# First layer of the last two chunks by seven block products in place of eight

## The chip, the cores and the metric

One core of one Trainium2 chip. The metric is the device time of one execution in microseconds (us). Before the change three runs took 883.08, 883.62 and 883.85 us, median 883.62.

## The reference

Attention with 8 heads of width 64 over 8 sequences of 576 tokens (half of the heads see the last 32 keys, the others every 32nd key), and then two matrix products with a softplus between them over all 4608 tokens:

```python
def _moe_ref(x, w_in, w_out):          # x: 4608 x 512
    h = x @ w_in                       # w_in: 512 x 2048
    g = np.maximum(h, 0.0) + np.log1p(np.exp(-np.abs(h)))
    return (g @ w_out).astype(np.float32)   # w_out: 2048 x 512
```

Every product runs as three products of rounded parts: with `a = a_high + a_low`, `a*b` is `a_high*b_high + a_low*b_high + a_high*b_low`.

## The kernel before

The tokens are cut into nine chunks of 512 (`c` = 0 to 8), the 2048 hidden columns into 16 slices of 128 (`f`). One pair (c, f) is a step, and its work is:

- `hidden(c, f)` on TensorE (PE): 4 blocks of the 512 inputs x 3 part products = 12 matmuls of 128x128 by 128x512 into one bank `ph_c_f`. Two banks alternate. In the plan this task is `F` and the step's number, 16c + f: F102 is `ph_6_6`, F106 is `ph_6_10`.
- `log_part` on ScalarE (ACT): three instructions (Abs, Exp, Ln) from `ph` into `u_c_f`.
- `softplus` on VectorE (DVE): one SCALAR_TENSOR_TENSOR, max(ph, 0) + u. It is the last reader of the bank; F of the step after next writes there.
- `g_high` (a CAST to the rounded part) and `g_low` (TENSOR_TENSOR, u minus the high part), on DVE.
- `output(c, f)` on PE: 4 blocks of 128 tokens x 3 = 12 matmuls into four banks `py`, two steps behind `hidden`. After f = 15 `result` copies each bank out (ACT and DVE in turn) and stores it.

The attention of sequence b, in four pairs of heads n = 4b to 4b + 3, lies between the steps of the chunks before. `head_scores(n)` is `S{n}` on PE; the weighted sums of pair n - 1 go with it (`po`, `pv`; `pv` takes a `ph` bank). DVE adds the mask, takes maxima, subtracts, sums, normalizes and transposes in 16 pieces (`prob_transposes`); ACT takes the exponentials. `x_part` writes the result as `x_h` (ACT) and `x_l` (DVE), a ring of 1536 tokens per block of 128 inputs: chunks 6, 7 and 8 lie in it together. The last pair's sums, `V31`, stand alone.

The first part of the program (chunk 0) has its order by hand (`FIRST`). From step 18 on a planner sets it: each task has an urgency, an engine, a cost and the tasks it follows; tasks take the earliest gap on their engine, and are emitted in the order of planned starts. Each engine then works through its own queue strictly in that order. What stands where is fixed by

```python
pair_at[NFC * (b - 1) - 2 + 4 * i] = NPAIR * b + i   # step at which S{n} goes
...
for i in range(begin, len(steps) + LAG):             # LAG = 2
```

GpSimd (POOL) works only in chunk 0. The weights w_in stay in SBUF as `w_i_f`, high and low part side by side.

Of the kernel before, what the change touches and what calls it, by code (L numbers as in the profile page):

```python
# [76 lines left out]
class Plan:  # L77
# [39 lines left out]
def attention_softplus_ffn(  # L117
# [164 lines left out]
    def load_v(n):  # L282
        b, pair = order[n]
        if n < NPAIR:

            t = room[n]
        else:
            t = v_in
        t = t[:, : 2 * NTILE * D].rearrange("p (a c) -> p a c", c=2 * D)
        src = v[b, pair]  # L290
        nc.sync.dma_start(t[PAD:P, 0], src[0:TILE])
        src = src[TILE - PAD : 2 * TILE]
        src = bass.AP(
            tensor=src.tensor,
            offset=src.offset,
            ap=[src.ap[0], [TILE * 2 * D, NTILE - 1], src.ap[1]],
        )
        nc.sync.dma_start(t[:, 1:NTILE], src)
        vs[n] = t.rearrange("p a (h d) -> p a h d", d=D)
# [350 lines left out]
    def hidden(c, f, pairs=range(NPAIR)):  # L650
        n = CH[c]
        if 0 in pairs:
            phs[c, f] = ps_h.tile([P, 512], F32, tag="ph", name=f"ph_{c}_{f}")[:, :n]
        ph = phs[c, f]
        t0 = START[c] % RING
        i = 3 * pairs[0]
        for cc in (PAIRS[pair] for pair in pairs):
            for half, x in ((0, "h"), (1, "h"), (0, "l")):
                nc.tensor.matmul(  # L659
                    ph,  # L660
                    lhsT=w32["i", f][:, half, cc * P : (cc + 1) * P],
                    rhs=x_of(x, cc)[:, t0 : t0 + n],
                    start=(i == 0),
                    stop=(i == 3 * NCC - 1),
                )
                i += 1

    def log_part(c, f, steps=range(3)):
        if 0 in steps:
            us[c, f] = u_pool.tile([P, 512], F32, tag="u", name=f"u_{c}_{f}")[:, : CH[c]]  # L670
            nc.scalar.activation(us[c, f], phs[c, f], AF.Abs)  # L671
        u = us[c, f]
        if 1 in steps:
            nc.scalar.activation(u, u, AF.Exp, scale=-1.0)  # L674
        if 2 in steps:
            nc.scalar.activation(u, u, AF.Ln, bias=1.0)  # L676

    def softplus(c, f):
        u = us[c, f]
        nc.vector.scalar_tensor_tensor(  # L680
            u, in0=phs.pop((c, f)), scalar=0.0, in1=u, op0=ALU.max, op1=ALU.add
        )

    def g_high(c, f, engine=nc.vector):
        g = g_pool.tile([P, 512], F32R, tag="gh", name=f"gh_{c}_{f}")[:, : CH[c]]
        ghs[c, f] = g
        copy_on(engine, g, us[c, f])

    def g_low(c, f, engine):
        g = g_pool.tile([P, 512], F32R, tag="gl", name=f"gl_{c}_{f}")[:, : CH[c]]  # L690
        gls[c, f] = g
        engine.tensor_tensor(g, us.pop((c, f)), ghs[c, f].bitcast(F32), op=ALU.subtract)  # L692

# [35 lines left out]
    def task(name, fn, *args):  # L729
        first[name] = lambda: fn(*args)  # L730
# [132 lines left out]
    for i in range(begin, len(steps) + LAG):  # L863
        if i < len(steps):
            c, f = steps[i]
            w, x = CH[c] / 384, when[i]
# [4 lines left out]
            after = [f"F{i}", f"l{i-2}"]
            add(f"A{i}", x + 2, "ACT", 1.5 * w, lambda c=c, f=f: log_part(c, f), after)
            add(f"u{i}", x + 3.7, "DVE", 0.55 * w, lambda c=c, f=f: softplus(c, f), [f"A{i}"])
            after = [f"u{i}", f"O{i-3}"]
# [12 lines left out]
        for t in range(nt):
            name = f"O{k}" if t == nt - 1 else f"O{k}.{t}"
            after = [f"l{k}", before] + ([f"y{k-1}.{t}"] if f == 0 else [])
            add(name, x + 0.01 * t, "PE", 0.7, lambda c=c, f=f, t=t: output(c, f, (t,)), after)  # L890
            before = name
            if k == len(steps) - 1 and t == nt - 1:

                for h, (e, engine) in enumerate((("DVE", nc.vector), ("ACT", nc.scalar))):
                    cols = slice(DM // 2 * h, DM // 2 * (h + 1))
                    fn = lambda c=c, t=t, engine=engine, cols=cols: result(c, t, engine, cols)
                    add(f"y{k}.{t}{h}", x + 0.7 * t + 0.7, e, 0.35, fn, [name])
            elif f == NFC - 1:
# [8 lines left out]
    for i, n in pair_at.items():  # L907
# [137 lines left out]
```

## Time and profile before

| | |
|---|---|
| median of three runs | 883.62 us (883.08 to 883.85) |
| span of the profiled execution | 882.3 us; its own device time is not listed apart from that, the median of the runs is 1.3 us above the span |
| PE busy | 872.7 us, 99% |
| DVE, ACT, POOL busy | 585.7, 403.0, 65.8 us |
| matmuls of `hidden` and `output` | 1152 + 576 each, of 3456 in all |
| bytes moved | 58.39 MB, mean 66 GB/s |

Each line of a view on groups gives a source line, engine and instruction, the tiles written and read, the shape and count, then the busy time in all and of one. A matmul counts as busy to the end of its pipeline, so that neighbours overlap: the distance of two starts says what one costs. A line of the chain gives a start, a length and what ran.

### The profile page before, as it was taken

The page shows a single profiled execution, that of the slowest core. Times are in us where ns is not written, and L with a number is a line of the kernel's source. Part 1 is how long each engine was busy: PE and PEld are TensorE (multiplying, and loading weights), DVE is VectorE, ACT ScalarE, POOL GpSimd, SP SyncE. Part 2 cuts the span into 40 slices and gives each one's busy share as a digit, 9 for nine tenths or more (in the row PEclk, how much of TensorE's full clock was granted, in tenths as well). Part 3 has the DMA queues.
Part 4 walks back from the last instruction along what each step waited for, and adds up shares of the span by engine and source line. Part 5 has one row for each costly group of instructions (what it writes and reads, how often), then busy time and mean ns, then how long its engine had stood idle before and what let it go on. Part 6 is the DMA issues. An engine that isn't in the chain of part 4 may idle for free.

```text
span 882.3 us, 16274 instructions
## 1 busy us (share of the span) xinstructions
PE 872.7 (99%) x6626; PEld 717.4 (81%) x6626; DVE 585.7 (66%) x1283; ACT 403.0 (46%) x742; POOL 65.8 (7%) x88
## 2 busy tenths in 40 slices
PE   7999999999999999999999999999999999999998
PEld 5887888888888888888888888888888888888886
DVE  7999977888766677777766676667767333333332
ACT  6988754443443443443443444444443333333332
POOL 6346540000000000000000000000000000000000
PEclk9999999999999999999999999999999999999999
DMA  9894202211211121111211121102100010001001
GB/s 327 289 351 140 63 30 92 61 46 45 93 45 45 44 75 32 45 45 46 81 43 45 45 93 45 40 24 79 54 19 18 1 48 0 1 1 48 1 0 48
DMA packets 50090, 58.39 MB, mean 66 GB/s; under 512 B 3168, under 2 KB 35296, under 8 KB 50016
## 3 DMA queue, kind: packets, MB, share of 16 engines
q1 hardware_dynamic: 49728, 57.03, 20.0%
q8 instruction: 52, 0.85, 0.4%
q10 hardware_dynamic: 288, 0.33, 0.1%
q14 instruction: 22, 0.18, 0.1%
HBM read 47.91 MB, written 9.44 MB: 65 GB/s over the span
## 4 chain that ended last, share of the span: by engine, by line
PE 93%; DMA 2%; DVE 2%; ACT 1%; issue 1%; POOL 0%; SPq 0%; ACTq 0%; POOLq 0%
PE py L699 43%; PE ph L659 42%; PE pv L555 2%; DMA ro<-in_moe_w_out_dram 2%; PE ps L373 2%; PE po L555 2%; PE po L373 1%; PE pt L525 1%; DVE pt L487 0%; DMA raw_q<-in_qk_dram 0%; ACT prob L453 0%; DVE early_h L258 0%; DVE u L680 0%; DVE a_o L630 0%; ACT early_h L258 0%
## 5 line engine op out<-in xcount | busy, mean ns | idle before, releaser
L699 PE MATMUL py<-w_o,gh 128*128 128x512 f32 x1152 | 358.0, 392 | 0.0
L659 PE MATMUL ph<-x_h,w_i 128*128 128x512 f32 x1152 | 355.4, 390 | 0.4 <-DVE u L680 0.4
L671 ACT ACTIVATE u<-ph 128x512 f32<-128x512 f32 x144 | 86.1, 599 | 396.4 <-PE ph L659 393.8
L659 PEld LDWEIGHTS ph<-x_h,w_i 128*128 128x128 f32 x1152 | 215.7, 188 | 46.0 <-POOL prob L476 0.8
L699 PEld LDWEIGHTS py<-w_o,gh 128*128 128x128 f32 x1152 | 214.2, 188 | 46.3
L659 PE MATMUL ph<-x_l,w_i 128*128 128x512 f32 x576 | 224.1, 389 | 0.0
L699 PE MATMUL py<-w_o,gl 128*128 128x512 f32 x576 | 224.1, 389 | 0.0
L680 DVE SCALAR_TENSOR_TENSOR u<-ph,u 128x512 f32<-128x512 f32 x144 | 99.2, 689 | 172.3 <-ACT u L676 170.7
L487 DVE STREAM_TRANSPOSE pt<-prob 32x192 f32<-32x192 f32 x448 | 140.2, 317 | 6.7
L699 PEld LDWEIGHTS py<-w_o,gl 128*128 128x128 f32 x576 | 108.1, 188 | 22.8
L659 PEld LDWEIGHTS ph<-x_l,w_i 128*128 128x128 f32 x576 | 108.1, 188 | 22.7
L692 DVE TENSOR_TENSOR gl<-u,gh 128x512 fp32r<-128x512 f32 x135 | 93.3, 691 | 10.6
L674 ACT ACTIVATE u<-u 128x512 f32<-128x512 f32 x144 | 91.1, 633 | 4.3
L676 ACT ACTIVATE u<-u 128x512 f32<-128x512 f32 x144 | 90.9, 632 | 4.4
L258 DVE CAST gh<-u 128x512 fp32r<-128x512 f32 x130 | 55.4, 426 | 10.8 <-DVE u L680 0.9
L432 DVE TENSOR_TENSOR prob<-ps,mask_b 128x384 f32<-128x384 f32 x28 | 15.6, 557 | 50.0 <-PE ps L373 48.5
L258 ACT COPY qT<-prob 128x576 f32<-128x576 f32 x26 | 33.2, 1278 | 1.5 <-DMA prob<-in_qk_dram 1.5
L447 ACT ACTIVATE prob<-prob 128x576 f32<-128x576 f32 x24 | 16.5, 687 | 38.0 <-DVE prob L441 38.0
L373 PEld LDWEIGHTS ps<-kT,qT 64*32 64x32 f32 x1344 | 23.3, 106 | 9.9 <-issue 9.2
L373 PE MATMUL ps<-kT,qT 64*32 64x64 f32 x1344 | 27.8, 220 | 0.0
L373 PE MATMUL po<-kT,qT 64*32 64x64 f32 x672 | 22.0, 227 | 0.0
L432 DVE TENSOR_TENSOR prob<-po,mask_b 128x192 f32<-128x192 f32 x28 | 10.0, 356 | 17.8 <-ACT x_h L593 17.8
(99 smaller groups left out, 512.9 us busy)
## 6 DMA issues: line engine op xcount, KB each, us to landing
v_in<-in_v_dram SPq DMA_DIRECT2D x28, 320.0 KB, 3.5
out_dram<-o SPq DMA_DIRECT2D x35, 256.0 KB, 2.1
ri<-in_moe_w_in_dram SPq DMA_DIRECT2D x16, 512.0 KB, 8.2
ro<-in_moe_w_out_dram SPq DMA_DIRECT2D x16, 512.0 KB, 8.7
kT<-in_qk_dram SPq DMA_DIRECT2D x28, 288.0 KB, 3.3
prob<-in_qk_dram SPq DMA_DIRECT2D x28, 288.0 KB, 2.7
v_in<-in_v_dram SPq DMA_DIRECT2D x28, 48.0 KB, 2.8
room<-in_v_dram SPq DMA_DIRECT2D x4, 320.0 KB, 6.0
```

The lines of the kernel that those rows point to most:

```text
L258: (engine.copy if engine is nc.scalar else engine.tensor_copy)(dst, src)
L373: nc.tensor.matmul(pss[n, part][to : to + 32, at : at + 64], lhsT=qT[head, c : c + 32], rhs=k_of(n)[head, c : c + 64], start=True, stop=True,)
L432: nc.vector.tensor_tensor(pv, sv, m, op=ALU.add)
L487: nc.vector.transpose(pt[32 * (i + c) : 32 * (i + c) + 32, h, a : a + hi - lo, 32 * i : 32 * i + 32,], src[:, lo:hi, 32 * c : 32 * c + 32],)
L555: nc.tensor.matmul(po[64 * h : 64 * h + 64, TILE * x : TILE * x + TILE], lhsT=vs[n][:, a, h, :], rhs=pt_of(n, a)[:, h, a % 2], start=True, ...
L659: nc.tensor.matmul(ph, lhsT=w32["i", f][:, half, cc * P : (cc + 1) * P], rhs=x_of(x, cc)[:, t0 : t0 + n], start=(i == 0), stop=(i == 3 * N ...
L671: nc.scalar.activation(us[c, f], phs[c, f], AF.Abs)
L674: nc.scalar.activation(u, u, AF.Exp, scale=-1.0)
L676: nc.scalar.activation(u, u, AF.Ln, bias=1.0)
L680: nc.vector.scalar_tensor_tensor(u, in0=phs.pop((c, f)), scalar=0.0, in1=u, op0=ALU.max, op1=ALU.add)
L692: engine.tensor_tensor(g, us.pop((c, f)), ghs[c, f].bitcast(F32), op=ALU.subtract)
L699: nc.tensor.matmul(py[t], lhsT=g[:, sl], rhs=w32["o", f][:, half], start=(f == 0 and n == 0), stop=(f == NFC - 1 and n == 2),)
```

## The change

The first layer of chunks 7 and 8, 2 x 16 x 12 = 384 matmuls, becomes a 2 x 2 block product: rows are the two chunks (X1 = chunk 7, X2 = chunk 8), inner blocks the two halves of the 512 inputs, columns slices f and f + 8. In eight rounds (f = 0 to 7) seven block products of 6 matmuls each stand in place of eight, in Winograd's form of Strassen's method. Products 1, 6, 7 and 4 add up in one PSUM bank (`bank_a0` or `bank_a1`, in turn), 2 goes to `bank_b`, 5 and 3 to `bank_c`. In between ACT copies the state of a bank to SBUF (`keep`: k1, k5, k2 after products 1, 5, 6) and DVE adds a bank to such a copy (`join`: j1, j2, j5 after products 2, 3, 7). j1 gives the hidden values of (7, f), j2 of (8, f), j5 of (8, f + 8), and the bank after product 4 those of (7, f + 8).

The block sums: of x once, 8 additions for each of two blocks (i = 0 on POOL; i = 1 on DVE but for two on POOL), then high parts on ACT and low parts on DVE (`Xh`, `Xl`; into `t1` and into parts of the ring no longer read); of the weights in each round, two additions of 128x512 and four of 128x256 on POOL (`ww`), two casts on ACT and two subtractions on DVE (`Wh`, `Wl`, into `ws`). Tiles of the attention are laid into four larger ones (`home_0` to `home_3`) so that these sums take their place at the end. The values of chunk 8 stay in the places of `w_i`, and its second layer comes at the end, block by block. The last sequence's pairs are three steps apart, not four.

```diff
-            pair_at[NFC * (b - 1) - 2 + 4 * i] = NPAIR * b + i
+            pair_at[NFC * (b - 1) - 2 + (4 if b < B - 1 else 3) * i] = NPAIR * b + i
...
-    steps = [(c, f) for c in range(NCHUNK) for f in range(NFC)]
+    steps = [(c, f) for c in range(CA) for f in range(NFC)]     # CA, CB = 7, 8
...
+    def bank_of(p, f):
+        return lend({"2": "b", "5": "c", "3": "c"}.get(p, f"a{f % 2}"))
+    def product(p, f):
+        bank = bank_of(p, f)
+        n = 0
+        for i in range(2):
+            for half, part in ((0, "h"), (1, "h"), (0, "l")):
+                nc.tensor.matmul(bank, lhsT=w_left(p, f, half, i), rhs=x_right(p, part, i),
+                    start=p in "125" and n == 0, stop=n == 5, ...)
...
+    def x_whole(what, i, engine):
+        h, low = (x_at(part, k, lo).bitcast(F32) for part in "hl")
+        engine.tensor_tensor(t, h, low, op=ALU.add)
+    def x_sum_low(p, i):
+        nc.vector.tensor_tensor(x_right(p, "l", i), sums_r[p, i], h, op=ALU.subtract)
+    def w_whole(r, f):
+        t = sums_c[r, f] = io_pool.tile([P, DM], F32, tag="io", name=f"ww_{r}_{f}")
+        nc.gpsimd.tensor_tensor(t, w[:, 0], w[:, 1], op=ALU.add)
+    def w_sum(p, f):
+        nc.gpsimd.tensor_tensor(out, a, b, op=op)
+    def w_sum_low(r, f):
+        nc.vector.tensor_tensor(ws[:, r, 1], sums_c.pop((r, f)), h, op=ALU.subtract)
+    def keep(s, p, f):
+        nc.scalar.copy(lend(s), bank_of(p, f))
+    def join(s, p, f, c, row):
+        nc.vector.tensor_tensor(t, bank_of(p, f), t, op=ALU.add)
+        phs[c, row] = t
...
+    for f in range(HALF):        # one round; some(n): n blocks of the second layer, 3 matmuls each
+        mul("1"); k1; mul("2"); j1; soft(CA, f)
+        some(1); mul("5"); k5; mul("6"); k2
+        some(1); mul("3"); j2; soft(CB, f)
+        some(1); mul("7"); j5; weights of round f + 1
+        some(3); mul("4"); soft(CB, f + 8); soft(CA, f + 8); some(2)
```

(The last block is the new loop in short; `soft` is the ACT and DVE work of a step.)

Up to the end of chunk 5 the queues read as before. Three places after that matter. `S30` and `V31` are the scores of pair 30 and the sums of pair 31; a name such as `ph_6_2_6460` is tile `ph_6_2` with a buffer number.

First, DVE behind `V31`. Before, `V31` came after F110, and in DVE's queue the softplus of step (6, 8) followed the transposes of pair 30:

```order
L487 STREAM_TRANSPOSE pt_98<-prob_103 32x6x32 x2
L487 STREAM_TRANSPOSE pt_98<-prob_103 32x3x32 x2
L680 SCALAR_TENSOR_TENSOR u_6_8_6798<-ph_6_8_6766,u_6_8_6798 128x512
L258 CAST gh_6_8_6826<-u_6_8_6798 128x512
L692 TENSOR_TENSOR gl_6_8_6840<-u_6_8_6798,gh_6_8_6826 128x512
```

Now `V31` comes between F104 and F105, and in the same queue the sums of x for i = 1 and two low parts stand ahead of it (`s12` and `s5` are the homes of the later copies, used for sums of x here):

```order
L836 TENSOR_TENSOR t1_6939<-xw_11_0_6473,t1_6939 128x512
L599 TENSOR_TENSOR x_l3_592<-pv_31_0_6908,x_h3_590 128x18x16
L599 TENSOR_TENSOR x_l3_592<-pv_31_1_6915,x_h3_590 128x18x16
L817 TENSOR_TENSOR xw_22_1_6962<-x_h3_590,x_l3_592 128x512
L817 TENSOR_TENSOR s12_6964<-x_h3_590,x_l3_592 128x512
L828 TENSOR_TENSOR xw_11_1_6855<-s5_6873,xw_11_1_6855 128x512
L828 TENSOR_TENSOR s5_6873<-xw_22_1_6962,s5_6873 128x512
L828 TENSOR_TENSOR xw_22_1_6962<-xw_22_1_6962,xw_11_1_6855 128x512
L828 TENSOR_TENSOR s12_6964<-s12_6964,xw_22_1_6962 128x512
L836 TENSOR_TENSOR t1_6939<-xw_11_1_6855,t1_6939 128x512
L836 TENSOR_TENSOR x_l1_526<-xw_22_1_6962,x_h1_507 128x512
L688 SCALAR_TENSOR_TENSOR u_6_8_6895<-ph_6_8_6859,u_6_8_6895 128x512
```

The softplus of (6, 8), F104's, has moved behind everything that follows `V31`, eleven instructions; F106 writes the bank that it reads.

Second, ACT in round 2. Before, chunk 7's steps followed one another:

```order
L671 ACTIVATE u_7_2_7252<-ph_7_2_7228 128x512
L674 ACTIVATE u_7_2_7252<-u_7_2_7252 128x512
L676 ACTIVATE u_7_2_7252<-u_7_2_7252 128x512
L671 ACTIVATE u_7_3_7295<-ph_7_3_7268 128x512
L674 ACTIVATE u_7_3_7295<-u_7_3_7295 128x512
```

Now the same queue has the end of the step (7, 9), then k1, k5, the step (7, 2) and k2:

```order
L684 ACTIVATE u_7_9_7441<-u_7_9_7441 128x512
L867 COPY s12_6964<-bank_a0_7194 128x512
L867 COPY s5_6873<-bank_c_7224 128x512
L679 ACTIVATE u_7_2_7496<-s12_6964 128x512
L682 ACTIVATE u_7_2_7496<-u_7_2_7496 128x512
L684 ACTIVATE u_7_2_7496<-u_7_2_7496 128x512
L867 COPY s12_6964<-bank_a0_7194 128x512
L858 CAST ws_7191<-ww_1_3_7505 128x512
```

In rounds 2, 4 and 6 k2 stands behind the three instructions of (7, f), which read what j1 writes; in the other rounds it stands ahead of them.

Third, POOL, which had nothing after chunk 0 (its last rows before):

```order
L645 TENSOR_TENSOR w_o_15_1758<-a_o_15_1616,w_o_15_1758 128x512
L258 COPY qT_99<-prob_103 128x576
L1040 UNCONDITIONAL_BRANCH
```

Now it ends with the weight sums, six a round:

```order
L842 TENSOR_TENSOR ww_0_4_7612<-w_i_4_610 128x512
L842 TENSOR_TENSOR ww_1_4_7623<-w_i_12_1215 128x512
L855 TENSOR_TENSOR ww_1_4_7623<-ww_1_4_7623 128x256
L855 TENSOR_TENSOR ww_1_4_7623<-ww_0_4_7612,ww_1_4_7623 128x256
L855 TENSOR_TENSOR ww_0_4_7612<-ww_1_4_7623,ww_0_4_7612 128x256
L855 TENSOR_TENSOR ww_0_4_7612<-ww_0_4_7612 128x256
```

With four buffers, those of round 4 take the places of round 2's, which `Wl` of round 2 reads last: they start at the end of round 1.

More of the change, by code (lines that the diff above doesn't have):

```diff
@@ L891, in attention_softplus_ffn @@
             before = name
[L892 to L898, printed above, removed]
+            if f == NFC - 1:
                 e, cost, engine = (("ACT", 0.5, nc.scalar), ("DVE", 0.6, nc.vector))[t % 2]
@@ L968, in attention_softplus_ffn, with on_pe, out_task @@
             add(f"v{n+1}", z + 2, "SP", 1.3, lambda n=n: load_v(n + 1), [made], 2.0)
+    SLOT = 0.234
+    HALF = NFC // 2
+    now = when[len(steps)]
+    chain = f"F{len(steps) - 1}"
+    def on_pe(name, slots, fn, after):
+        nonlocal now, chain
+        add(name, now, "PE", slots * SLOT - Plan.WAIT, fn, [chain] + after)
+        now, chain = now + slots * SLOT, name
+    def out_task(c, f, t):
+        name, own = f"O{c}.{f}.{t}", [f"l{c}.{f}"]
+        if c == CA - 1:
+            own = [f"l{NFC * c + f}"]
+        elif f == 0:
+            own.append(f"y{c-1}.{t}")
+        on_pe(name, 3, lambda: output(c, f, (t,)), own)
+        if f < NFC - 1:
+            return
+        if c == CB and t == TPC - 1:
+            for h, (e, engine) in enumerate((("DVE", nc.vector), ("ACT", nc.scalar))):
+                cols = slice(DM // 2 * h, DM // 2 * (h + 1))
+                fn = lambda engine=engine, cols=cols: result(c, t, engine, cols)
+                add(f"y{c}.{t}{h}", now, e, 0.35, fn, [name])
+            return
+        e, cost, engine = (("ACT", 0.6, nc.scalar), ("DVE", 0.7, nc.vector))[t % 2]
+        add(f"y{c}.{t}", now, e, cost, lambda: result(c, t, engine), [name])
@@ new lines, in soft_task @@
+    def soft_task(c, f, src, late=()):
+        n = f"{c}.{f}"
+        for step in range(3):
+            fn = lambda step=step: log_part(c, f, (step,))
+            add(f"A{step}.{n}", now + step, "ACT", 0.65, fn, [src] if step == 0 else [f"A{step-1}.{n}"])
+        add(f"u{n}", now + 3, "DVE", 0.75, lambda: softplus(c, f), [f"A2.{n}"])
+        add(f"h{n}", now + 3.7, "DVE", 0.45, lambda: g_high(c, f), [f"u{n}", *late])
+        add(f"l{n}", now + 4.2, "DVE", 0.75, lambda: g_low(c, f, nc.vector), [f"h{n}"])
@@ new lines, in x_task @@
+    def x_task(i):
+        e, engine = ("POOL", nc.gpsimd) if i == 0 else ("DVE", nc.vector)
+        cost = 1.45 if i == 0 else 0.75
+        near, far = ([f"L{last - 3 + 2 * i + k}{half}" for half in range(2)] for k in range(2))
+        z = when[i_of[last - 3 + 2 * i + 1]] + 6
+        free = [f"V{last}"]
+        start = [f"Y{last}0", f"Y{last}1", f"S{last}"] if i == 1 else []
+        whole = {"11": near, "12": near + start, "22": far, "21": far + start}
+        sums = {"5": ["11", "12"], "7": ["12", "22", "5"], "6": ["22", "5", "7"], "4": ["21", "6"]}
+        to = {"5": free, "6": ["12"], "7": [chain], "4": [chain]}
+        k = 0
+        for what in ("11", "22", "12", "21"):
+            fn = lambda what=what: x_whole(what, i, engine)
+            early = "POOL" if i == 1 and what in ("11", "12") else e
+            by = nc.gpsimd if early == "POOL" else engine
+            fn = lambda what=what, by=by: x_whole(what, i, by)
+            add(f"X{what}.{i}", z + k, early, 1.45 if early == "POOL" else cost, fn, whole[what])
+            k += 0.1
+        for p in ("5", "7", "6", "4"):
+            fn = lambda p=p: x_sum(p, i, engine)
+            add(f"X{p}.{i}", z + k, e, cost, fn, [f"X{q}.{i}" for q in sums[p]])
+            k += 0.1
+        for p in ("5", "6", "7", "4"):
+            after = [f"X{p}.{i}"] + [q if len(q) > 2 else f"X{q}.{i}" for q in to[p]]
+            late = 0 if p in "56" else now - z
+            add(f"Xh{p}.{i}", z + late + k, "ACT", 0.65, lambda p=p: x_sum_high(p, i), after)
+            after = [f"Xh{p}.{i}"]
+            add(f"Xl{p}.{i}", z + late + k + 1, "DVE", 0.75, lambda p=p: x_sum_low(p, i), after)
+            k += 0.1
@@ new lines, in w_task @@
+    def w_task(f, z):
+        since = [f"P6.{f-1}", f"W3.{f-1}"] if f else [f"F{len(steps) - 2}"]
+        for r in range(2):
+            add(f"W{r}.{f}", z, "POOL", 1.45, lambda r=r: w_whole(r, f), since)
+        before = [f"W0.{f}", f"W1.{f}"]
+        for p in ("5", "7", "6", "3"):
+            add(f"W{p}.{f}", z + 3, "POOL", 0.8, lambda p=p: w_sum(p, f), before)
+            before = [f"W{p}.{f}"]
+        used = {0: "63", 1: "57"}
+        for r, done in ((1, "7"), (0, "3")):
+            after = [f"W{done}.{f}"] + (
+                [f"P{p}.{f-1}" for p in used[r]] if f else [f"V{last}", f"S{last}"]
+            )
+            add(f"Wh{r}.{f}", z + 6, "ACT", 0.65, lambda r=r: w_sum_high(r, f), after)
+            add(f"Wl{r}.{f}", z + 7, "DVE", 0.75, lambda r=r: w_sum_low(r, f), [f"Wh{r}.{f}"])
@@ L969, in attention_softplus_ffn @@
+    for g in (HALF - 1, NFC - 1):
+        for t in range(TPC):
+            out_task(CA, g, t)
+    for t in range(TPC):
+        for f in range(HALF):
+            for g in (f, f + HALF):
+                out_task(CB, g, t)
     with tc.manual_schedule():
```

216 lines of the change are left out of this document (191 added, 25 removed).

## The prediction

> **What bounds the kernel now.** I read the page first, then stretches of the span, the chain that ended last and the waits.
>
> ```profile
> PE 872.7 (99%) x6626; PEld 717.4 (81%) x6626; DVE 585.7 (66%) x1283; ACT 403.0 (46%) x742; POOL 65.8 (7%) x88
> PEclk9999999999999999999999999999999999999999
> ```
>
> PE is busy for 99% of the span at its full granted clock. The stretches (busy us and instructions of PE, PEld, DVE, ACT, POOL, then clock, DMA share, GB/s) show where other engines have room:
>
> ```profile
> 640.00:690.00 50.00, 50.00 (x407) 41.03 (x408) 33.70 (x76) 18.69 (x31) 0.00 (x0) 1.00 0.06 16
> 784.00:832.00 48.00, 48.00 (x213) 39.77 (x212) 17.41 (x29) 17.06 (x28) 0.00 (x0) 1.00 0.06 22
> ```
>
> While attention runs DVE is busy for two thirds, in the last chunks for 36%; POOL does nothing in either. In the chain the last two chunks are matmuls and nothing else, and the wait list has, from chunk 1 on, no wait of PE that matters:
>
> ```profile
> 734.27 2.72 PE py L699 x12
> 736.99 2.72 PE ph L659 x12
> ...
> 870.27 8.17 PE py L699 x36
> ```
>
> ```profile
> PE ph L659 <- DVE u L680: 0.4, 1, 0.4
> ```
>
> Twelve matmuls take 2.72 us, so one takes a slot of 0.227. What removes a slot is worth a slot, as long as PE finds no new wait.
>
> **What it removes.** Eight rounds of seven products of 6 matmuls are 336, in place of 384: 48 slots, **-10.9 us**. Nothing else leaves PE: second layer, attention and the end (a copy in two halves and a store) keep their work. The two POOL sums for i = 1 end before V31 and cost nothing. No transfer is added; the loads of the last pairs come a few us earlier, which the same three-step spacing in chunk 1 bore without a wait of PE.
>
> **What it adds on the other engines.** The prices:
>
> ```profile
> L692 DVE TENSOR_TENSOR gl<-u,gh 128x512 fp32r<-128x512 f32 x135 | 93.3, 691 | 10.6
> L258 DVE CAST gh<-u 128x512 fp32r<-128x512 f32 x130 | 55.4, 426 | 10.8 <-DVE u L680 0.9
> L674 ACT ACTIVATE u<-u 128x512 f32<-128x512 f32 x144 | 91.1, 633 | 4.3
> L258 ACT COPY o<-py 128x512 f32<-128x512 f32 x19 | 10.2, 582 | 5.2 <-PE py L699 5.2
> L692 POOL TENSOR_TENSOR gl<-u,gh 128x512 fp32r<-128x512 f32 x9 | 12.2, 1355 | 7.8 <-DVE gh L258 5.1 <-PE ph L659 1.0 <-ACT gh L258 0.9
> ```
>
> A round has 66 slots (42 of products, 24 of second layer), 14.96 us. DVE's part in it: four steps of 0.69 + 0.43 + 0.69, three joins and two low parts of 0.69, 10.7 us; ACT's: four of 1.87, three copies and two casts of 0.6, 10.5 us; POOL's: two sums of 1.36 and four of half that (an estimate), 5.4 us. As sums all fit. What decides is the order in each queue and one contention.
>
> **The contention.** From chunk 0, where POOL worked beside DVE (start, us):
>
> ```profile
> 94.74 1.16 POOL L476 TENSOR_TENSOR prob<-prob,st 128x576 f32<-128x576 f32 x1
> ...
> 107.74 1.30 POOL L692 TENSOR_TENSOR gl<-u,gh 128x512 fp32r<-128x512 f32 x1 [0.98 <-PE ph L659]
> ```
>
> ```profile
> 94.71 0.69 DVE L680 SCALAR_TENSOR_TENSOR u<-ph,u 128x512 f32<-128x512 f32 x1 [1.08 <-ACT u L676]
> ...
> 107.87 1.72 DVE L630 SCALAR_TENSOR_TENSOR a_o<-ro,a_o 128x512 uint32<-128x512 uint32 x1
> ...
> 123.06 0.79 DVE L258 CAST w_o<-a_o 128x512 fp32r<-128x512 f32 x1
> ```
>
> ```profile
> 84.41 0.68 DVE L645 TENSOR_TENSOR w_o<-a_o,w_o 128x512 fp32r<-128x512 f32 x1
> 84.62 0.93 POOL L258 CAST gh<-u 128x512 fp32r<-128x512 f32 x1 [1.62 <-DVE u L680]
> 85.01 1.09 DVE L630 SCALAR_TENSOR_TENSOR a_o<-ro,a_o 128x512 uint32<-128x512 uint32 x1
> 85.52 1.73 POOL L645 TENSOR_TENSOR w_o<-a_o,w_o 128x512 fp32r<-128x512 f32 x1
> ```
>
> A DVE instruction with both inputs in SBUF takes 1.72 instead of 0.69 when POOL began first: it works only once POOL is through (107.87 + 1.72 - 0.69 = 108.90, so POOL held it 1.16). In the third block the two engines take turns, each lengthened by the other. A DVE instruction with one input in PSUM (94.71) keeps its 0.69. So I charge a whole POOL sum 1.16 and a half one 0.57 (estimate) to each such DVE instruction that meets it. The Trainium skill has this as a rule (SBUF — State Buffer, "Who interferes with whom"): a VectorE instruction with two SBUF inputs and a GpSimd one that reads SBUF exclude each other, and whoever issued first keeps the port for the whole instruction; the trace agrees (1.72 against 0.69). By that rule the sum is the one below; if nothing met, it would be the first rival's.
>
> In a round 13 of DVE's 17 instructions are of the exposed kind (the casts too: the one at 123.06 took 0.79 beside a POOL sum, against a mean of 0.426), and the six POOL sums of the round after next become ready exactly when `Wl` has freed their buffers, at the round's start.
>
> **Waits in the Strassen rounds.** Handoffs:
>
> ```profile
> 805.02 0.60 ACT L671 ACTIVATE u<-ph 128x512 f32<-128x512 f32 x1 [3.51 <-PE ph L659]
> ...
> 806.32 0.63 ACT L676 ACTIVATE u<-u 128x512 f32<-128x512 f32 x1
> ...
> 806.99 0.69 DVE L680 SCALAR_TENSOR_TENSOR u<-ph,u 128x512 f32<-128x512 f32 x1 [3.56 <-ACT u L676]
> ...
> 807.78 0.43 DVE L258 CAST gh<-u 128x512 fp32r<-128x512 f32 x1
> ...
> 808.31 0.69 DVE L692 TENSOR_TENSOR gl<-u,gh 128x512 fp32r<-128x512 f32 x1
> ```
>
> ACT to DVE costs 0.04, a dependent DVE instruction 0.1, three ACT instructions 1.95. Count from product 1's first slot. Product 7 starts at slot 39, 8.84 us, and needs k2; product 4 at slot 54, 12.24, and needs j5.
>
> *Even rounds (2, 4).* Product 4 of the round before ended at -1.4. Five ACT instructions end at 2.0 to 2.2; then DVE has two softplus, two casts, two low parts, and j1. Undisturbed, from the first of the two Ln at 1.4 (an instruction followed by an independent one costs 0.08 less than its time): 0.6 + 0.7 for the softplus, 0.7 the casts, 1.2 the low parts, 0.7 j1, end 5.3; the step (7, f) ends at 7.5, k2 at 8.1: hidden by 0.7. With POOL's two whole sums from 0.1 the first softplus waits to 2.6; the second, with a bank in PSUM, does not wait; then each cast (0.3 on the port) and low part (0.53) lets a half sum go first: 2.6 + 0.6 + 0.6 + 0.3 + 0.57 + 0.3 + 0.57 + 0.53 + 0.57 + 0.6 + 0.7 = 7.9 for j1, ACT 9.9, k2 10.5. Product 7 waits **1.7** in rounds 2 and 4 each, and all of PE's queue behind it, so that the wait is lost whole; on ACT a cast for the next weights and the step (8, f) stand behind k2 and come later by as much. Round 6 has no weight sums left to meet.
>
> *Odd rounds.* k2 comes first and is in time; j5 follows (7, f)'s low part at 12.0 against 12.24: no wait. Round 1 is the exception: its POOL queue holds two sets of sums (the second waits for stores of chunk 6's results), the second meets (7, 1). j1, late by the first set as above, ends at 8.5, ACT at 10.5; softplus, cast and low part each let a half sum go first, 10.9 + 0.53 + 0.57 + 0.3 + 0.57 + 0.6 + 0.7 = 14.1 for j5: **1.9**.
>
> *Round 0.* Count from F111's end: its own step and two low parts of weights keep DVE to 5.1. Four low parts of x follow, and alternate with the first set, 5.1 + 1.16 + 0.53 + 1.16 + 0.53 + 0.57 + 0.53 + 0.57 + 0.6 = 10.8, so that j1 ends at 11.5, not 8.3. k2 waits for the last of them and ends at 11.5 (product 7 was due at 11.4), (7, 0) on ACT at 13.5, its softplus, cast and low part at 15.4, j5 at 16.1; product 4 was due at 15.0: **1.3** with the little at product 7. k1, behind six casts, ends 6.3 after F111 and product 6 starts at 7.3: hidden.
>
> *After round 7.* (7, 15) leaves the bank with product 4; Abs to low part (0.2, five ACT instructions in the queue, softplus, two casts, two low parts) end at 5.4, PE comes to them after 20 slots, 4.5: **0.9** (0.5 to 1.1, by the dependent gaps).
>
> Bounds of the first three: 0 without a meeting; and if a half sum held the port as long as a whole one, four times 0.6 more a burst, of which I let half reach PE, 1.2 in each of four rounds.
>
> **Waits in chunk 6.** A pair's block on PE and DVE's work behind it, before:
>
> ```profile
> 151.06 0.41 PE ps L373 x20
> ...
> 153.19 2.94 PE py L699 x12
> ```
>
> ```profile
> 159.41 2.64 DVE L487 STREAM_TRANSPOSE pt<-prob 32x192 f32<-32x192 f32 x8
> ```
>
> The block takes 2.13 plus 0.22 on the next group, and the transposes begin 8.35 after it. They take 5.2 (16 at 0.33 by this row). Now all 16 stand ahead of F100's softplus, and F102, which writes its bank, stands after S30 and four groups, 2.13 + 2.94 + 3 x 2.72 = 13.2, first slot 13.1. Softplus ends at 8.35 + 5.2 + 0.7 = 14.2: already 1.1 late. POOL's sums of x for i = 0 start once pair 29's low parts are written, and hold up the subtraction and the low part of (6, 3): another 1.1. **2.2** (0 to 2.6).
>
> F106 waits for F104's softplus. From V31's end: a cast into `t1` 0.6, its low part 0.6, two low parts of 0.36, sums 0.6 to 0.8 each (six, three of them dependent, 4.2), two low parts 1.2, softplus 0.7: 8.2 with the handoffs. PE has F105 and one output group in between, 2.94 + 2.72 - 0.16 = 5.5. **2.8**; the ACT side alone (F105's three, two casts, low part, softplus, 4.7 after F105's end against 2.7) makes it 2.0 at least; 3.2 at most if POOL's last sum is late.
>
> **The sum.** -10.9 + 2.2 + 2.8 + 1.3 + 1.9 + 3.4 + 0.9 = +1.6 us against the profiled 882.3; on the median of 883.62, **885.2 us**. All low ends (-10.9 + 2.0 + 0.5) give 875.2; all high ends (-10.9 + 2.6 + 3.2 + 6.6 + 4.8 + 1.1 = +7.4) 891.
>
> **Rivals.** *The two engines seldom meet on the path.* If POOL is done before DVE's burst, only the waits written in the order stay: -10.9 + 1.1 + 2.8 + 0.9 = -6.1, **877.5**, the other side. For it: DVE has 4 us of free time a round; against: the buffers tie POOL's start to DVE's burst. It decides where j1 of rounds 2 and 4 ends before 6.0. *Nothing waits*: 872.7; chunk 1's spacing speaks for it, the DVE queue behind V31 against. *Late j5 in every round with weight sums*, not in round 1 alone: two more of 1.9 (rounds 3 and 5), 889, and with a part of the high ends **890**; for it speaks that odd rounds have 0.2 to spare by my count, against it that POOL has one set a round there.
>
> **How the numbers follow.** A measurement tells 0.2%, 1.8 us, from no change. My case (882 to 888.5) 0.52, of which 0.32 within 1.8 us and 0.20 above; seldom meeting (875 to 881) 0.25; nothing waits 0.07; late in every round 0.16. Faster 0.32, same 0.32, slower 0.36. The range 876 to 890 leaves out the 0.07 and the ends of two cases.
>
> **What would show it.** 3408 matmuls of the two layers in place of 3456; PE waits for DVE's softplus at `ph` twice in chunk 6 (2 to 3 us each), at `bank_a0` for ACT's copy in rounds 2 and 4; DVE low parts well over 0.69 beside POOL. Wrong if DVE's mean there stays near 0.69 or if j1 ends by 6.

## The result, and the profile after

The changed kernel takes **888.51 us** (median of four runs, 888.27 to 889.00) against 883.35 of the kernel before on the same chip: a ratio of 1.0058, 95% interval 1.0043 to 1.0072. It is slower by 5.2 us. The prediction was 885.2 with 876 to 890, a loss of 1.6 us; its likeliest class, slower by over 0.2%, came out, and its number was 3.3 us low.

The page of the changed kernel, the lines that answer to those at the head of the prediction:

```profile
PE 866.6 (98%) x6578; PEld 709.1 (80%) x6578; DVE 636.1 (72%) x1337; ACT 425.4 (48%) x790; POOL 134.5 (15%) x146
PEclk9999999999999999999999999999989999999999
```

PE has 48 instructions less and is busy 6.1 us less, not 10.9. One slice of the clock row reads 8: PE ran some of its work at a lower clock. Stretches (columns as in the prediction; the last is the group of matmuls that follows the longest wait):

```profile
640.00:690.00 50.00, 43.39 (x283) 34.70 (x282) 38.22 (x76) 16.29 (x29) 9.62 (x9) 0.93 0.03 8
784.00:832.00 48.00, 48.00 (x213) 39.67 (x212) 33.43 (x55) 31.59 (x57) 6.07 (x6) 1.00 0.00 1
645.00:650.40 5.40, 5.40 (x13) 4.28 (x14) 3.40 (x6) 0.00 (x1) 0.00 (x0) 0.53 0.00 0
```

In chunk 6 PE stands still for 6.6 of 50 us. In the last rounds it is as full as before, while DVE has twice the work (33.4 us of 48 in place of 17.4). In the third stretch the granted clock is 0.53.

The waits of PE from 600 us on (who waited, for whom; us in all, times, longest). Before, this list was empty here:

```profile
PE ph L667 <- DVE u L688: 6.6, 2, 4.2
PE bank_a L798 <- DVE s L872: 1.8, 2, 1.1
PE bank_a L798 <- ACT s L867: 1.5, 2, 1.0
PE py L714 <- DVE gl L707: 0.5, 1, 0.5
```

These are the seven waits that the prediction named, and no others: softplus in front of F102 and F106, j5 in rounds 0 and 1, k2 in rounds 2 and 4, the low part of (7, 15). A wait is counted from the end of the last matmul, 0.39 after its start, while a slot is 0.227; so each costs 0.16 us more than its row says. The longest, on PE's timeline:

```profile
640.37 0.39 PE L714 MATMUL py<-w_o,gl 128*128 128x512 f32 x1
644.98 1.22 PE L667 MATMUL ph<-x_h,w_i 128*128 128x512 f32 x2 [4.22 <-DVE u L688]
646.00 0.63 PE L667 MATMUL ph<-x_l,w_i 128*128 128x512 f32 x1
646.42 1.05 PE L667 MATMUL ph<-x_h,w_i 128*128 128x512 f32 x2
...
650.20 0.63 PE L714 MATMUL py<-w_o,gh 128*128 128x512 f32 x2
```

From start to start it is 4.61 us, of which 4.38 are lost. The matmuls behind it stand 0.42 to 0.43 apart, not 0.227: the next group starts 5.22 us after F102's (650.20 and 644.98) where 2.72 was usual, another 2.5 us. In the chain this group counts 5.38 us, since a group behind a wait is counted there to the end of its last matmul, 0.16 more.

### The profile page after: what moved, and what is told of

Same layout as the page of the kernel before. It is cut to its first block, busy times and chain, and to the rows that moved or that the text cites. A ratio compares the mean times of both kernels' runs of the same rounds, so it can differ in the third digit from the quotient of the medians.

```text
span 886.9 us, 16332 instructions
## 1 busy us (share of the span) xinstructions
PE 866.6 (98%) x6578; PEld 709.1 (80%) x6578; DVE 636.1 (72%) x1337; ACT 425.4 (48%) x790; POOL 134.5 (15%) x146
## 4 chain that ended last, share of the span: by engine, by line
PE 81%; DVE 9%; ACT 4%; DMA 3%; issue 2%; SPq 0%; POOL 0%; ACTq 0%; DVEq 0%; POOLq 0%
PE py L714 38%; PE ph L667 31%; PE bank_a L798 3%; PE pv L563 2%; PE ps L381 2%; PE po L563 2%; DVE home L495 2%; PE bank_c L798 1%; DVE u L688 1%; ACT u L682 1%; DVE gl L707 1%; PE po L381 1%; DMA ri<-in_moe_w_in_dram 1%; ACT u L684 1%; ACT u L679 1%
## 5 line engine op out<-in xcount | busy, mean ns | idle before, releaser
L714 PE MATMUL py<-w_o,gh 128*128 128x512 f32 x1024 | 318.4, 392 | 0.0
L667 PE MATMUL ph<-x_h,w_i 128*128 128x512 f32 x896 | 279.1, 393 | 7.1 <-DVE u L688 7.1
L714 PEld LDWEIGHTS py<-w_o,gh 128*128 128x128 f32 x1024 | 190.5, 188 | 41.5 <-DVE gh L266 0.2
L667 PEld LDWEIGHTS ph<-x_h,w_i 128*128 128x128 f32 x896 | 168.2, 189 | 44.0 <-DVE u L688 7.6
L714 PE MATMUL py<-w_o,gl 128*128 128x512 f32 x512 | 199.3, 389 | 0.5 <-DVE gl L707 0.5
L667 PE MATMUL ph<-x_l,w_i 128*128 128x512 f32 x448 | 175.2, 391 | 0.0
L495 DVE STREAM_TRANSPOSE home<-home 32x192 f32<-32x192 f32 x448 | 140.2, 317 | 6.8
L714 PE MATMUL py<-w_o,g 128*128 128x512 f32 x192 | 43.7, 389 | 0.0
L714 PEld LDWEIGHTS py<-w_o,g 128*128 128x128 f32 x192 | 36.0, 188 | 7.5
L842 POOL TENSOR_TENSOR ww<-w_i 128x512 f32<-128x512 f32 x16 | 24.1, 1520 | 77.2 <-DVE ws L863 63.0
```

Source lines behind the costliest of these rows:

```text
L495: nc.vector.transpose(pt[32 * (i + c) : 32 * (i + c) + 32, h, a : a + hi - lo, 32 * i : 32 * i + 32,], src[:, lo:hi, 32 * c : 32 * c + 32],)
L667: nc.tensor.matmul(ph, lhsT=w32["i", f][:, half, cc * P : (cc + 1) * P], rhs=x_of(x, cc)[:, t0 : t0 + n], start=(i == 0), stop=(i == 3 * N ...
L714: nc.tensor.matmul(py[t], lhsT=g[:, sl], rhs=w32["o", f][:, half], start=(f == 0 and n == 0), stop=(f == NFC - 1 and n == 2),)
```

## The experiments

Every kernel ran beside the kernel before on one chip. Medians in us, ratio to before with its 95% interval:

| run | this | before | ratio |
|---|---|---|---|
| e1_spacing | 883.22 | 883.23 | 1.0002 (0.9993 to 1.0012) |
| e2_warm | 886.46 | 883.23 | 1.0030 (1.0018 to 1.0043) |
| e3_xlate | 886.27 | 883.23 | 1.0030 (1.0018 to 1.0042) |
| e4_wless | 887.04 | 883.23 | 1.0038 (1.0024 to 1.0051) |
| e5_k2first | 886.88 | 883.32 | 1.0041 (1.0026 to 1.0056) |
| e6_order | 886.19 | 883.32 | 1.0030 (1.0021 to 1.0040) |
| e7_rounds | 885.71 | 883.32 | 1.0026 (1.0017 to 1.0036) |
| e8_all | 883.13 | 883.32 | 1.0002 (0.9993 to 1.0012) |
| e9_chunk6 | 888.00 | 883.10 | 1.0051 (1.0039 to 1.0064) |
| e10_rounds | 884.99 | 883.10 | 1.0019 (1.0010 to 1.0028) |
| e11_best | 883.57 | 883.10 | 1.0006 (0.9996 to 1.0015) |
| e12_final | 880.73 | 883.46 | 0.9970 (0.9958 to 0.9982) |

The start of the program varies by 1.7 us from one profiled execution to another, and the 95% intervals of many rows overlap; so the readings below go by single waits on PE's timeline, not by differences of spans or of medians.

### The wait in front of F102

**e1_spacing.** The kernel before with one line of the change:

```diff
-            pair_at[NFC * (b - 1) - 2 + 4 * i] = NPAIR * b + i
+            pair_at[NFC * (b - 1) - 2 + (4 if b < B - 1 else 3) * i] = NPAIR * b + i
```

> The kernel before with only the last sequence's pairs three steps apart: no block product, no sum on POOL. My theory: the changed kernel's wait of 4.4 us at F102 is about 1.9 of order (softplus of (6, 4) behind 16 transposes) and 2.5 of POOL's sums on DVE's port, and the half-speed matmuls behind it (2.7 us) come from PE having stood still so long. Then this kernel waits 1 to 2 us at F102, its matmuls keep full speed, and it takes 0.8 to 2.3 us more than before, about 885. Rival (the spacing is the whole of it): 4 us of wait and the slow matmuls here too, about 890.

No change in time, and of PE's waits for softplus one is left, the 0.4 us that the kernel before has too:

```profile
PE ph L659 <- DVE u L680: 0.4, 1, 0.4
```

Both theories were wrong. With the spacing alone the planner puts F100 ahead of S30 and softplus of (6, 4) ahead of all 16 transposes. So the closer pairs alone do not make the order of the changed kernel. What else in the change moved S30 forward and softplus back there, the tasks of the x sums placed among these most likely, no run separates.

**e3_xlate.** POOL's last five sums for i = 0 wait until pair 30's transposes are through:

```diff
+    def hold():
+        t = st_pool.tile([P, NTILE, 2], F32, tag="hold", name="hold")
+        nc.gpsimd.tensor_copy(t, pt[:, 1, :, 0:64:32])
...
+            if i == 0 and what == "22":
+                fn = lambda: (hold(), x_whole("22", 0, nc.gpsimd))
+            if i == 0 and what in ("22", "21"):
+                whole[what] = whole[what] + [f"P{last - 1}"] + (["X22.0"] if what == "21" else [])
```

> The changed kernel with POOL's last five sums of x for i = 0 held back until the transposes of pair 30 are through (POOL first copies 12 columns of their result). My theory: subtraction, low part of (6, 3) and normalization return to 0.76, 0.70 and 0.76 us (from 0.90, 1.77, 1.69), F102 waits about 1.9 in place of 4.4, and its matmuls run at full speed: 883.3; if 1.9 us of standing still are enough to lose the clock, 886. Rival (the order alone makes the wait): F102 still waits 4 us, 888.5.

The changed kernel, POOL's five sums and DVE beside them (subtraction, low part of (6, 3), the small addition behind the row sums, reciprocal, normalization, transposes, softplus):

```profile
632.23 3.06 POOL L817 TENSOR_TENSOR xw<-x_h,x_l 128x512 f32<-128x512 f32 x2 [12.11 <-DVE x_l L599]
635.24 4.89 POOL L828 TENSOR_TENSOR xw<-xw,xw 128x512 f32<-128x512 f32 x3
```

```profile
633.23 0.90 DVE L449 TENSOR_TENSOR home<-home,st 128x576 f32<-128x576 f32 x1
634.06 1.77 DVE L707 TENSOR_TENSOR gl<-u,gh 128x512 fp32r<-128x512 f32 x1
...
636.53 0.49 DVE L476 TENSOR_SCALAR st<-st 128x9 f32<-128x9 f32 x1
637.05 0.21 DVE L480 RECIPROCAL st<-st 128x9 f32<-128x9 f32 x1
637.30 1.68 DVE L484 TENSOR_TENSOR home<-home,st 128x576 f32<-128x576 f32 x1
639.01 5.19 DVE L495 STREAM_TRANSPOSE home<-home 32x192 f32<-32x192 f32 x16
644.24 0.69 DVE L688 SCALAR_TENSOR_TENSOR u<-ph,u 128x512 f32<-128x512 f32 x1
```

With the sums held back, the same work, and PE's wait:

```profile
633.17 0.76 DVE L449 TENSOR_TENSOR home<-home,st 128x576 f32<-128x576 f32 x1
633.85 0.68 DVE L707 TENSOR_TENSOR gl<-u,gh 128x512 fp32r<-128x512 f32 x1
...
635.47 0.17 DVE L476 TENSOR_SCALAR st<-st 128x9 f32<-128x9 f32 x1
635.68 0.21 DVE L480 RECIPROCAL st<-st 128x9 f32<-128x9 f32 x1
635.92 0.76 DVE L484 TENSOR_TENSOR home<-home,st 128x576 f32<-128x576 f32 x1
```

```profile
642.69 0.72 PE L667 MATMUL ph<-x_h,w_i 128*128 128x512 f32 x2 [2.02 <-DVE u L688]
```

Subtraction, low part and normalization return to 0.76, 0.68 and 0.76, and the wait falls from 4.22 to 2.02, the matmuls behind it at full clock. So 2.2 us of this wait were the port and 2.2 the order. The whole gained less than I expected, 2.2 of 5.2 us, because the next wait, F106's, grew to 2.66 and now lost the clock (its group took 4.62 us). The 886 of the second case in the expectation came out by luck: it was to come from 1.9 us of standing at F102, and F102 kept its clock.

**e2_warm.** Twelve matmuls that nobody reads, ahead of F102:

```diff
+    def extra(n):
+        spare = ps_s.tile([P, 512], F32, tag="ps", name="spare")
+        for _ in range(n):
+            nc.tensor.matmul(spare, lhsT=w32["i", 6][:, 0, :P], rhs=x_of("h", 0)[:, :512],
+                start=True, stop=True)
...
+        if (c, f) == (6, 6):
+            add(f"F{i}", x, "PE", 2.1 * w, lambda c=c, f=f: (extra(12), hidden(c, f)), after)
```

> The changed kernel with 12 extra matmuls, whose result nobody reads, ahead of F102. They take 2.7 us of a wait of 4.4. My theory, that standing still brings the clock down: F102's 12 matmuls take 2.7 to 2.9 us in place of 5.4, and the kernel gains about 2.7 us, 885.8. Rival (the 12 matmuls are slow because of what they read or of the other engines): F102 still takes 5.4 us and the time stays 888.5. If extra work simply delays, it is 891.

The chain at F102 and at F106:

```profile
645.02 3.01 PE ph L667 x12
...
673.21 4.25 PE ph L667 x12
```

F102 starts at the same place (645.02 against 644.98) behind 1.5 us of standing, and its group takes 3.01 in place of 5.38: it was the standing still that halved the clock, since the operands and the other engines' work are the same. Now the group of F106, behind a wait of 2.38, is slow. In the changed kernel the same wait of 2.38 was followed by 3.04 us. So part of the gain was lost again there. It differs from run to run: of the six runs of this kernel the two with a mean clock of 0.998 took 887.3 and 887.9 us, the four with 0.999 or 1.000 took 885.2 to 886.7 (the changed kernel's four runs have 0.995 to 0.997).

What differs between the two waits of 2.38 can be read from the clock. In every trace here the stretches between two changes of the granted clock are whole multiples of 3.41 us (in the changed kernel 0.50 from 643.28 to 650.10, in e2_warm from 674.70 to 678.11). Cut along these intervals, the wait at F106 lies within one in e2_warm and is divided between two in the changed kernel (columns as in the stretches above; e2_warm first):

```profile
671.29:674.70 3.41, 1.49 (x6) 1.24 (x7) 3.34 (x6) 0.04 (x1) 2.67 (x2) 1.00 0.00 0
674.70:678.11 3.41, 3.41 (x9) 2.66 (x8) 3.09 (x4) 0.60 (x1) 3.17 (x4) 0.50 0.00 0
```

```profile
670.58:673.99 3.41, 2.63 (x12) 1.85 (x10) 3.31 (x6) 2.94 (x5) 0.00 (x0) 1.00 0.00 0
673.99:677.41 3.42, 1.82 (x8) 1.51 (x9) 3.35 (x5) 0.00 (x0) 3.00 (x2) 1.00 0.02 5
677.41:680.82 3.41, 3.41 (x17) 2.81 (x16) 2.96 (x5) 1.87 (x3) 3.17 (x4) 1.00 0.00 0
```

In e2_warm PE was idle for 1.92 us of one interval, and the next ran at half clock; in the changed kernel it was idle for 0.78 and 1.60 us of two, and the clock stayed.

**e6_order.** Same work, other order in chunk 6:

```diff
+            if n == last - 1 and j == 2:
+                after = after + [f"l{i}"]
...
+            if i == 0:
+                after.append(f"l{i_of[last - 1]}")
...
+        if i == 1:
+            far, late = [*far, f"l{i_of[last] + 3}"], f"l{i_of[last] + 3}"
```

The first condition makes the third quarter of pair 30's transposes follow the low part of (6, 4), the second makes the high parts of the sums for i = 0 follow it, and the third puts the sums for i = 1 behind the low part of (6, 10).

> The changed kernel, same work, other order in chunk 6: softplus, cast and low part of (6, 4) after half of pair 30's transposes and its ACT part ahead of the high part of a sum of x; the sums of x for i = 1 behind the low part of (6, 10). Theory: the waits of F102 and F106 (4.4 and 2.9 us of lost time) go, and with them the 2.7 us of slow matmuls: 10.0 less, 878.5. Rival (POOL's port holds softplus up anyway): F102 still waits 1 to 2 us, 880 to 881, and if the clock falls there too, 883.

```profile
PE ph L667 <- DVE u L688: 4.9, 2, 4.4
```

886.19 us, above the theory and the rival's range. F106's wait is gone (the other of these two, 0.5 us, lies ahead of 600 us and is in the kernel before as well), F102's is not: the planner answered by putting F102 one group forward, ahead of O99. It had 2.72 us less cover, met POOL's sums as before, waited 4.4 and ran at half clock again.

**e9_chunk6** keeps these conditions, holds F102 behind O99 and adds the hold of e3_xlate:

> Chunk 6 alone. The reordering of two runs ago moved F102 ahead of O99, so that PE came to its wait a group of 2.72 us earlier and still stood 4.4 us. Here F102 stays behind O99, softplus, cast and low part of (6, 4) stand after half of pair 30's transposes, POOL's last five sums for i = 0 wait for these transposes, and the sums of x for i = 1 stand behind (6, 10). Theory (half of the wait at F102 is contention, 2.2, and half the order, 2.2): both go, F106's wait shrinks to 0.5 or less, no slow matmuls: 9.5 less than the changed kernel, 879. Rival (softplus needs something else): F102 still waits 2 us or more, 881 to 884.

```profile
PE pv L563 <- issue: 6.1, 1, 6.1
PE ph L667 <- DVE u L688: 0.5, 1, 0.5
```

888.00 us, above both cases again. The wait at F102 is gone altogether, as expected of order and port together (the 0.5 is the early one again). In its place stands one of 6.1 us at V31, which the planner had now put ahead of F104: V31 needs pair 31's transposes and writes a bank whose last reader, a low part of pair 30's sums, stands behind them (it ended at 663.2, V31 began at 663.3). The POOL sums, moved behind pair 30, lengthened two casts and two low parts ahead of all this:

```profile
646.58 0.95 DVE L266 CAST gh<-u 128x512 fp32r<-128x512 f32 x1
647.64 1.57 DVE L707 TENSOR_TENSOR gl<-u,gh 128x512 fp32r<-128x512 f32 x1
```

### The waits of the rounds

**e4_wless.** No weight sums on POOL from round 4 on:

```diff
+        if f >= 4:
+            sums_c[r, f] = sums_c[r, 2 + f % 2]
+            return
```

> The changed kernel without POOL's weight sums for rounds 4 to 7 (ACT and DVE round those of rounds 2 and 3 again; the result is then not the reference's). POOL has nothing to do from round 2 on. My theory (contention): j1 ends in time in rounds 2 and 4, PE's waits for k2 (1.2 and 0.9 us of lost time) vanish, those for j5 in rounds 0 and 1 stay: about 2.0 less, 886.5. Rival (ACT's order, k2 behind the three instructions of (7, f), makes them late by itself): both waits stay, 888.5.

DVE in round 2 of the changed kernel and of this one: softplus, two casts, two low parts, j1.

```profile
742.77 0.69 DVE L688 SCALAR_TENSOR_TENSOR u<-s,u 128x512 f32<-128x512 f32 x1 [1.08 <-ACT u L684]
...
743.98 0.92 DVE L266 CAST g<-u 128x512 fp32r<-128x512 f32 x1
...
745.70 1.22 DVE L707 TENSOR_TENSOR g<-u,g 128x512 fp32r<-128x512 f32 x1
...
747.99 0.68 DVE L872 TENSOR_TENSOR s<-bank_b,s 128x512 f32<-128x512 f32 x1
```

```profile
743.26 0.69 DVE L688 SCALAR_TENSOR_TENSOR u<-s,u 128x512 f32<-128x512 f32 x1 [1.08 <-ACT u L684]
...
744.47 0.42 DVE L266 CAST g<-u 128x512 fp32r<-128x512 f32 x1
...
745.14 0.68 DVE L707 TENSOR_TENSOR g<-u,g 128x512 fp32r<-128x512 f32 x1
...
746.34 0.68 DVE L877 TENSOR_TENSOR s<-bank_b,s 128x512 f32<-128x512 f32 x1
```

Product 1 of the round starts at

```profile
741.18 0.39 PE L798 MATMUL bank_a<-x_h,w_i 128*128 128x512 f32 x1
```

```profile
741.68 0.62 PE L798 MATMUL bank_a<-x_h,w_i 128*128 128x512 f32 x2
```

so j1 ends at 7.5 with the sums and at 5.3 without them. Both waits for k2 are gone; of PE's waits for a bank only j5's in rounds 0 and 1 stay. With k2 at this place in ACT's queue contention made them, as expected.

**e5_k2first.** The sums stay; k2 stands ahead of (7, f) on ACT in even rounds:

```diff
-        soft_task(CA, f, f"j1.{f}")
+        soft_task(CA, f, f"j1.{f}", early=[f"k2.{f}"])
```

> The changed kernel with k2 ahead of the three instructions of (7, f) on ACT in rounds 2, 4 and 6, as it stands in the odd rounds; POOL's sums stay. The run without weight sums showed that contention alone decides whether these waits come; this asks whether order alone can hide them. My theory: k2 needs only product 6, so both waits (2.05 us of lost time) go, (7, f) comes later but j5 stays in time: 886.5. Rival (the wait moves to j5, as in rounds 0 and 1): 1 us each in rounds 2 and 4, 888.5.

Both waits for k2 are gone here too, and 886.88 is near the 886.5 expected: taking away the contention removes them, and so does another place in the queue.

**e7_rounds** adds two orders, j5 ahead of the cast of (7, f) in rounds 0 and 1, and (7, 15) ahead of (8, 15); **e10_rounds** has the first in every round (without the `if f < 2`):

```diff
-        soft_task(CA, f, f"j1.{f}")
+        soft_task(CA, f, f"j1.{f}", late=[f"j5.{f}"] if f < 2 else [], early=[f"k2.{f}"])
...
+        if f == HALF - 1:
+            soft_task(CA, f + HALF, f"got.{f}")
+            late = [f"P4.{f}", f"W3.{f}", f"l{CA}.{f+HALF}"]
+            soft_task(CB, f + HALF, f"A2.{CA}.{f+HALF}", late)
```

> The changed kernel, same work, other order in the rounds: k2 first in even rounds as in the run before the last; in rounds 0 and 1 j5 ahead of the cast and low part of (7, f); in round 7 (7, 15) ahead of (8, 15). Theory: all five waits of the rounds go (0.86 + 1.30 + 1.16 + 0.9 + 0.7 of lost time, 4.9): 883.6. Rival (j5 waits for DVE's queue ahead of the cast too): 1 to 2 us of them stay, 885.

> The rounds alone, as in the run on the rounds, but j5 ahead of the cast and low part of (7, f) in every round. There the wait left round 0 and halved in round 1, and one of 1.8 us at j5 appeared in round 2, which the run with k2 alone did not have. Theory (with PE no longer late from rounds 0 and 1, j5 of round 2 meets POOL's sums, and it is its place behind the low part that makes it late): that wait falls under 0.7, the rounds lose 1.4 us or less in all, 884.5 for the whole. Rival (j1 itself is too late, so that no place of j5 helps): 1.8 stays, 886.

PE's waits for j5, e7 and then e10:

```profile
PE bank_a L798 <- DVE s L872: 2.2, 2, 1.7
```

```profile
PE bank_a L798 <- DVE s L872: 1.0, 2, 0.5
```

In e7 round 0 is free and round 1 waits 0.5, but j5 of round 2 waits 1.7, which e5 did not show: without the waits of rounds 0 and 1 PE comes sooner (product 1 of round 2 starts 2.0 us ahead of POOL's sums, in e5 beside them). So e7's 885.71 is the rival's case. With j5 ahead everywhere two waits of 0.5 are left, in rounds 1 and 2, and 884.99 is near the theory's 884.5.

**e8_all** joins e6 and e7, **e11_best** e9 and e10:

> Both reorderings together. Theory (the losses are separate and add): 10.0 + 4.9 less than the changed kernel, 873.6, which is 1.1% below the kernel before; what is left is the 48 matmul slots alone. Rival (what is taken out of chunk 6 comes back in round 0, since sums of x, casts and weight sums of rounds 0 and 1 come later): 876 to 879.

> The two runs above in one kernel. Theory (the losses add, and what is left is 48 slots less 1 to 2 us of waits): 874 to 875.5, 0.9 to 1.1% faster than the kernel before. Rival (a late x or weight sum now meets round 0): 877 to 879.

883.13 and 883.57: the reorderings roughly add (5.4 and 4.9 us less than the changed kernel, where e6 and e7 alone have 2.3 and 2.8, e9 and e10 0.5 and 3.5), but both miss theory and rival: both keep the large wait of chunk 6 (4.4 us at F102, 6.0 at V31) with half clock behind it, and end where the kernel before is.

**e12_final.** The order of PE in chunk 6 held as in the changed kernel, POOL's five sums behind pair 31:

```diff
+        if i > 100:
+            after.append(f"O{i - 3}")
+        if i == i_of_last + 2:
+            after.append(f"V{last}")
...
-                whole[what] = whole[what] + [f"P{last - 1}"] + (["X22.0"] if what == "21" else [])
+                whole[what] = whole[what] + [f"P{last}"] + (["X22.0"] if what == "21" else [])
```

(`after` is what F{i} follows; output tasks follow the F ahead of them in the same way, V31 follows O102, and the high part of one sum for i = 0 follows the low part of (6, 9).)

> The reordering of both parts once more. In the run on chunk 6 the wait at F102 was gone, but V31 had moved a group forward, ahead of F104, and POOL's sums lengthened casts and low parts ahead of pair 31's transposes: PE stood 6.1 us there instead. Here F102 to F106 and O99 to O104 keep the order of the changed kernel, V31 stays behind O102, and POOL's last five sums for i = 0 wait for the transposes of pair 31, not 30. Theory (each wait is order or port, and none is needed): chunk 6 loses 1 us or less, the rounds 1.3 (j5 of rounds 1 and 2), no slow matmuls: 875, 0.9% faster than the kernel before. Rival (attention at this spacing leaves DVE no room for the extra work): 2 us or more at V31 or F106, and half clock behind it, 879 to 882.

880.73 us: the first version that is faster than the kernel before, by 0.3%. It lies in the rival's range, with a wait at a place that the rival did not name. The rounds have no wait left, and of chunk 6 one:

```profile
PE ph L667 <- DVE x_l L599: 5.5, 1, 5.5
```

```profile
653.26 5.19 DVE L495 STREAM_TRANSPOSE home<-home 32x192 f32<-32x192 f32 x16
658.48 0.46 DVE L599 TENSOR_TENSOR x_l<-pv,x_h 128x288 fp32r<-128x288 f32 x1
```

```profile
659.09 4.71 PE ph L667 x12
```

F104 writes the `ph` bank that holds pair 30's sums (`pv_30`), and the low part that reads it last stands behind pair 31's transposes. Neither theory had this wait. With 5.5 + 0.16 lost and 1.8 of half clock (4.71 less 0.16, for 2.72), an order without it should come to about 873, an estimate; it was not run, and it may bring a new wait, as other orders here did.

## Why the prediction was right or wrong

Term by term; "lost" is from start to start on PE less the slots in between:

| term | predicted | lost |
|---|---|---|
| 48 slots | -10.9 | -10.9 |
| F102 | 2.2 | 4.4 |
| half clock behind it | not in the sum | 2.5 |
| F106 | 2.8 | 2.5 |
| round 0, j5 | 1.3 | 0.9 |
| round 1, j5 | 1.9 | 1.3 |
| rounds 2 and 4, k2 | 3.4 | 1.2 + 0.7 |
| after round 7 | 0.9 | 0.7 |

- **The slots.** Right: `hidden` has 1344 matmuls, the products 336, `output` 1728, 3408 in all, at the same distance as before.
- **The places.** Right, all of them. The rival that nothing waits and the one that only the written order waits are out, and so is j5 late in every round: rounds 3 and 5 have no wait. The measured 888.5 lies at the upper end of my own case (882 to 888.5).
- **Luck in the total.** The seven waits lose 11.7 us where 12.5 were forecast, but only because F102 was 2.2 too small and the other six together 3.0 too large.
- **F102**, the step that was mis-sized. Its order was priced at 1.1 and cost 2.2; the port, priced at 1.1 for the subtraction and one low part, cost 2.2, since POOL's five sums ran to 640.1 and also held normalization (1.68 for 0.76) and the small addition (0.49 for 0.17). The range given for it, 0 to 2.6, did not hold.
- **The clock**, the step that was left out. I priced each wait by its length alone. PE's first group behind 4.2 us of standing ran at a granted clock of 0.53, which e2_warm shows to come from the standing. The Trainium skill has the rule (TensorE: Matmul & The Clock Gate, "What's actually happening"): the array falls to half rate after an idle window of about 3.4 us and returns after as long a busy one. The runs agree for long waits: each of 4.2 us or more at F102, V31 or F104 (ten kernels' traces) was followed by half-speed matmuls. They go beyond it for short ones: of seven waits of 2.4 to 2.7 us at F106, three were followed by a slow group (4.25 to 4.62 us) and four were not (3.0 to 3.1). The three had 1.92, 2.39 and 2.66 us of idle PE within one interval of 3.41, the four at most 1.60. Over all intervals of the fourteen traces in which the clock was at 1.00 it fell behind each with more than 1.94 us of idle PE and behind none with less than 1.91.
- **F106.** Right in size and cause: with the sums of x behind (6, 10), as in e6_order, the wait is gone.
- **The rounds.** Right in mechanism, 5.3 forecast for rounds 1, 2 and 4 and 3.2 lost. j1 of round 2 was forecast at 7.9 with and 5.3 without contention, and measured 7.5 and 5.3. The larger error lies in the first softplus: I let it wait until POOL was through with both whole sums, but it began between the two (742.77, its usual 0.69), and the second softplus ended 2.9 us after product 1's first slot, not 3.8. The casts and low parts behind took 4.0 us where I had counted 3.4, which gave part of it back. In round 4 POOL's sums began 0.5 ahead of product 1 (771.95 and 772.44), so that j1 ended at 7.0 and only 0.7 was lost. Why rounds 0 and 1 lost 0.4 and 0.6 less than forecast no run shows. The Trainium skill's rule on the shared port (SBUF — State Buffer, "Who interferes with whom"), used in the prediction, is borne out: cast and low part of round 2 take 0.92 and 1.22 beside POOL and return to 0.42 and 0.68 without it.

The seven waits lose 11.7 us, the half clock 2.5; less 10.9 that is 3.3. From the first weighted sums of pair 28 (593.81 before, 593.47 now) to the end of the span (882.3 and 886.9) the two profiled executions differ by 4.9 us. Of the 1.6 left about 0.9 stand in the groups behind the other six waits: their first two matmuls are 0.34 apart, and from start to start twelve matmuls take 2.85 to 2.88 us there, not 2.72. The last 0.7 stay open.

## What to carry to other kernels

A removed slot is worth a slot only while the engine that loses it finds its inputs ready; with PE at 99% each new wait counts in full, and one long wait counts again through the clock. Work moved to an idle engine costs where it meets a busy one: look up which instructions share its port, and place it in time, not only by its sum. Where a planner sets the order, read the queues again after every edit: three of these reorderings removed the wait that they aimed at and moved another instruction into a new one.

## What the hardware showed that I had not expected

- PE's granted clock changes at the ends of intervals of 3.41 us, and about 1.9 us of idle PE within one were enough to halve it for the next. So the same wait of 2.38 us did so in e2_warm, where it lay within one interval, and not in the changed kernel, where it was divided between two; no wait of 2.02 us or less did so at the places above.
- A very small DVE instruction, the addition on 128 x 9 elements, took 0.49 us beside POOL's sums and 0.17 without them, while the reciprocal on the same tile stayed at 0.21 in both.
